# Seven block products for eight in the gate projection of four groups: a fused cosformer attention and SwiGLU kernel

## The chip, the cores and the metric

The kernel runs on one core of a Trainium2 chip. The time is device microseconds (us) of one execution, as the median of several runs. A profile of one execution stands beside it.

## The reference

Linear attention with cosine weights for 8 batches, 8 heads, 576 tokens and a head size of 64, followed by a gated feed-forward block of width 1536. In short:

```python
def phi(x, c, s):                      # c, s: cos and sin of pi/2 * position / 576
    r = np.maximum(x, 0.0)
    return np.concatenate([r * c, r * s], axis=-1)
kv  = einsum('bhsf,bhsd->bhfd', phi(k), v)
z   = sum over s of phi(k)
x   = einsum('bhsf,bhfd->bhsd', phi(q), kv) / (einsum('bhsf,bhf->bhs', phi(q), z) + 1e-6)
x   = x, heads side by side            # 4608 tokens x 512
g   = x @ w_gate                       # 512 x 1536
out = (g * sigmoid(g) * (x @ w_val)) @ w_out
```

All inputs and the output are float32.

## The kernel before

**Tiling.** The 4608 tokens go in nine groups (`tg` 0 to 8) of 512 tokens (T), each of four tiles of 128 tokens. For each group the kernel makes the normalised attention output x of four tiles, turns it into xT (512 features in four chunks of 128, tokens along the free axis), computes gate and value for twelve blocks of 128 hidden features (`fc` 0 to 11), and then the output projection of the group. x is held 4096 times too large (UP), and DOWN takes this out in silu and in the last copies.

**Engines.** Each engine executes its own queue strictly in the order in which the code issues instructions (`tc.manual_schedule`). Waits between engines follow from the data they share: PSUM banks, tiles, DMAs.

- TensorE: gate and value projections (`ffn_mm`, L535, eight matmuls of 512 columns for a block), the output projection, attention tiles (`a_tile2`, L419) and the sums over keys (`kv_mm`, L305).
- ScalarE: silu (`ffn_silu`, L541), relu of q and k (L238), some copies.
- VectorE: gate times value (`ffn_mul`, L546, into `ht`), the normalisation of a tile (`x_den`, `x_rec`, `x_mul`: L429, L438, L442), phi of q (`phi_q`, L255), weighted v (`vmul`, L259), copies.
- SP issues the transposing DMAs of q (`qturn_dma`) and of x to xT (`x_turn`, L519), and the stores. POOL issues the loads.

**The output projection** of groups 2 to 8 (`out_by_quarters`) is already done with seven block products for eight (Winograd's form): tokens and output features are halved, hidden features are split into the even and odd blocks, so each operand has four quarters. Four sums of weight quarters (`weight_sum`, T1 to T4) are made once, four sums of token quarters (`token_sum`, S1 to S4, L623) for each group. The seven products accumulate into banks a, b, c and e. b starts as ScalarE's copy of a; e goes to SBUF as C22; c starts as VectorE's sum of C22 and b.

**PSUM.** `take` and `give_back` share out the eight banks in program order. A request for one bank (`n = 1`) or an aligned pair (`n = 2`, for tiles and `kv_mm`) gets the free one that was used longest ago:

```python
b0 = min(free, key=lambda b: (n == 1 and hold is not None and hold[0] == "o" and b ^ 1 not in taken,
                              sorted(used[b:b + n], reverse=True)))
```

A request held under a name that begins with "o" prefers a bank whose neighbour is taken. A bank may be given again at once after `give_back`; the next writer then waits on the chip for the engine that still reads it. [...]

**Slots.** A group after the first two has 16 slots: one behind each `fc` and one at each of the four `slot_of` calls of the output projection. A plan (`at`) puts the attention work of coming groups into these slots: the four phi of the next batch at output slots 0, 0, 1, 2; the four `vmul` from output slot 3 to slot 2 of the next group; `kv_mm` at slot 5; the next group's tiles with their transposes at slots 5, 7, 9 and 11. Batch work ends with group 6, tiles with group 7. Group 8 has neither.

Of the kernel before, what the change touches and what calls it, by code (L numbers as in the profile page):

```python
# [10 lines left out]
FP32 = mybir.dt.float32  # L11
# [3 lines left out]
ALU = mybir.AluOpType  # L15
# [3 lines left out]
def kernel(  # L19
# [28 lines left out]
    HC = FC // 2  # L48
    HT = T // 2
    HD = d_model // 2  # L50

    consts = ctx.enter_context(tc.tile_pool(name="consts", bufs=1))
    raw = ctx.enter_context(tc.tile_pool(name="raw", bufs=3))
    rel = ctx.enter_context(tc.tile_pool(name="rel", bufs=1))
    phip = ctx.enter_context(tc.tile_pool(name="phip", bufs=2))
    xp = ctx.enter_context(tc.tile_pool(name="xp", bufs=4))
    xtp = ctx.enter_context(tc.tile_pool(name="xtp", bufs=3))
    smp = ctx.enter_context(tc.tile_pool(name="smp", bufs=3))
    sgp = ctx.enter_context(tc.tile_pool(name="sgp", bufs=5))
    obp = ctx.enter_context(tc.tile_pool(name="obp", bufs=2))  # L60
    psum = ctx.enter_context(tc.tile_pool(name="psum", bufs=1, space=bass.MemoryType.PSUM))

# [10 lines left out]
    def take(n, hold=None, fills=False, seeded=False):  # L73

        taken = {x for r in held.values() for x in r}
        free = [b for b in range(0, 8, n) if not any(b <= x < b + n for x in taken)
                and (filled[b] or not seeded)]

        b0 = min(free, key=lambda b: (n == 1 and hold is not None and hold[0] == "o" and b ^ 1 not in taken,
                                      sorted(used[b:b + n], reverse=True)))  # L80
        if hold is not None:
            held[hold] = range(b0, b0 + n)
        filled[b0:b0 + n] = [fills or seeded] * n
        touch(range(b0, b0 + n))
        return banks[:, b0] if n == 1 else banks[:, b0:b0 + n]
# [15 lines left out]

    def raw_of(b, nm):
        if (b, nm) not in raws:
            raws[b, nm] = raw.tile([P, G, NC, D], BF16, name=f"raw_{nm}")
        return raws[b, nm]

    def load(b, nm, parts=1):
# [48 lines left out]
    ident = consts.tile([P, P], BF16)  # L156
    make_identity(nc, ident)
    kvd = []
    for j in range(2):
        t = consts.tile([P, 8 * J * D1], BF16, name=f"kvd_{j}")  # L160
        if j:
            nc.gpsimd.memset(t.bitcast(FP32), 0.0)
        kvd.append(t.rearrange("p (e j w i x) -> p e j w i x", e=2, j=J, w=2, i=2))


    zeros = consts.tile([P, P], BF16)
# [41 lines left out]
        in_=csk.rearrange("p c e -> p (c e)").to_broadcast([P, NC * 2, D]),  # L208
    )
    v2s = []  # L210
    for j in range(2):
        t = consts.tile([P, G, NC, 2, W], BF16, name=f"v2_{j}")
        nc.vector.tensor_copy(out=t[:, :, :, :, D], in_=csk.unsqueeze(1).to_broadcast([P, G, NC, 2]))
        v2s.append(t)


    wg_sb = consts.tile([P, KC, d_ff], BF16)
    wv_sb = consts.tile([P, KC, d_ff], BF16)
    wg_r = moe_w_gate.rearrange("(c p) f -> p c f", p=P)
    wv_r = moe_w_val.rearrange("(c p) f -> p c f", p=P)  # L220
    wo_r = moe_w_out.rearrange("(c p) f -> p c f", p=P)
# [35 lines left out]

    def vmul(b, g):
        nc.vector.tensor_tensor(  # L259
            out=v2s[b % 2][:, g, :, :, 0:D],  # L260
            in0=(first if b == 0 and g == 0 else {"v": raw_of(b, "v")})["v"][:, g].unsqueeze(2).to_broadcast([P, NC, 2, D]),
            in1=tab, op=ALU.mult,
        )
# [34 lines left out]
    def kv_mm(b):  # L298
        ps = st[b, "kvps"] = take(2, ("kv", b))
        for j, c in [(j, c) for j in range(J) for c in range(NC)]:  # L300
            for i in range(2):
                for e in range(2):
                    es = slice(e * SH, (e + 1) * SH)
                    g = 2 * j + i
                    nc.tensor.matmul(  # L305
                        out=ps[i * D:(i + 1) * D, e, j * 2 * D1:(j + 1) * 2 * D1],
                        lhsT=raws[b, "k"][es, g, c],
                        rhs=v2s[b % 2][es, g, c, :, 0:D1],
                        start=(c == 0), stop=(c == NC - 1),
                    )  # L310

# [47 lines left out]
            give_back(("kvf", j))  # L359


    qf = consts.tile([P, 2, J, 2, D], BF16)
    qr = [lodge(4 * J * SH, BF16).rearrange("p (e j c s) -> p e j c s", e=2, j=J, c=2) for i in range(2)]
    qwT = [lodge(8 * J * SH, BF16).rearrange("p (w e j c s) -> p w e j c s", w=2, e=2, j=J, c=2) for i in range(2)]

# [68 lines left out]
    def x_rec(t, ps, ys=slice(0, 4)):  # L434
        if ys.start == 0:
            st["rec", t] = smp.tile([P, H, 1], FP32, name="rec")
            st["x", t] = xp.tile([P, d_model], BF16, name="x")
        nc.vector.reciprocal(out=st["rec", t].rearrange("p (e y) o -> p e y o", e=2)[:, :, ys],  # L438
                             in_=st["den", t].rearrange("p (e y) o -> p e y o", e=2)[:, :, ys])

# [40 lines left out]
    def x_norm(t):  # L481
        num = st.pop(("num", t)).rearrange("p j e (i x) -> p (j e i) x", i=2)
        den = smp.tile([P, H, 1], FP32, name="den")
        nc.vector.tensor_scalar(out=den, in0=num[:, :, D:D1], scalar1=1e-6, scalar2=DOWN,
                                op0=ALU.add, op1=ALU.mult)
        rec = smp.tile([P, H, 1], FP32, name="rec")
        nc.vector.reciprocal(out=rec, in_=den)
        x = xp.tile([P, d_model], BF16, name="x")
        for j in range(J):
            hs = slice(4 * j, 4 * j + 4)  # L490
            nc.vector.tensor_tensor(
                out=x[:, 4 * j * D:(4 * j + 4) * D].rearrange("p (i e d) -> p e i d", i=2, e=2),
                in0=num[:, hs, 0:D].rearrange("p (e i) d -> p e i d", e=2),
                in1=rec[:, hs].rearrange("p (e i) o -> p e i o", e=2).to_broadcast([P, 2, 2, D]), op=ALU.mult,
            )
        st["x", t] = x

    def xT_of(t):
        tg, off = divmod(t, GH // 2)
        if tg not in xT:  # L500
            xT[tg] = xtp.tile([P, GH // 2, KC, P], BF16, name="xT")
        return xT[tg][:, off]

    def x_turn_pe(t, ks=slice(0, KC)):
        ps = take(1, ("xt", t, ks.start)).bitcast(BF16).rearrange("p (k x) -> p k x", x=P)
        for kc in range(ks.start, ks.stop):
            nc.tensor.transpose(out=ps[:, kc], in_=st["x", t][:, kc * P:(kc + 1) * P], identity=ident)  # L507
        st["xt", t, ks.start] = ps[:, ks]

    def x_turned(t, eng, ks=slice(0, KC)):  # L510
# [40 lines left out]
    def ffn_act(*a):  # L551
        ffn_silu(*a)
        ffn_mul(*a)

    def ffn_fc(*a):

        ffn_mm(*a)
        ffn_act(*a)

    out_v = out.rearrange("(b p c) f -> b c p f", p=SH, c=NC)  # L560
    o_ps = {}
# [68 lines left out]
    def out_by_quarters(tg, slot_of):  # L630
# [60 lines left out]
        if last:  # L691
            store_two(t0 + 2, slice(HD, d_model))
        product(c, aq[:, 1, 1], T4, False)
        copied("dve", C21, c)
        free("c")
        if last:
            store_two(t0 + 2, slice(0, HD))
# [178 lines left out]
    for b in range(2, B):  # L876
        s0 = SLOTS * (b - 1)
        keng = "dve" if b == 2 else "act"
        steps = [lambda b=b, g=g: phi_q(b, g) for g in range(G)]
        steps += [lambda b=b, g=g: (relu_k(b, g, g + 1, keng), vmul(b, g)) for g in range(G)]  # L880
        if b == 2:
            fs, tq = [s0 + i for i in (0, 0, 1, 1, 4, 5, 5, 6)], (s0 + 2, s0 + 2)
        else:
            p0 = s0 - SLOTS
            fs, tq = [p0 + 12, p0 + 12] + [p0 + 11 + i for i in range(2, 8)], (p0 + 15, p0 + 16)
            if b == 3:
                fs, tq = [p0 + 12 + i for i in range(4)] + [s0 + 4, s0 + 4, s0 + 5, s0 + 5], (s0 + 2, s0 + 2)
            at(p0 + 3 if b < 5 else p0 + 1, lambda b=b: load_behind(b))
        tk = (s0 + 4, s0 + {2: 8, 3: 7}.get(b, 5))
        for s, f in zip(fs, steps):  # L890
            at(s, f)
        for e in range(2):
            at(tq[e], lambda b=b, e=e: qturn_dma(b, e))
        at(tk[-1], lambda b=b: kv_mm(b), lambda b=b: kv_out2(b))
        at(tk[-1] + 1, lambda b=b: kv_free(b))
    for t in range(2 * OUT, NTG * OUT):
        tg, i = divmod(t, OUT)
        s = SLOTS * (tg - 1) + (5 if tg > 2 else 4) + 2 * i
        if t == 2 * OUT:
            at(s, a_(t, 0))  # L900
            at(s + 1, a_(t, 1), turn(t))
        elif tg == 2:
            at((9, 10, 11)[i - 1] + SLOTS, lambda t=t: a_tile2(t), turn(t))
            if i == 2:
                at(11 + SLOTS, load_3)
        else:
            if t in (13, 14, 15):
                s = SLOTS * 2 + t - 4
            at(s, lambda t=t: a_tile2(t), turn(t))
    for tg in range(1, NTG):  # L910
        s0 = SLOTS * tg
        for fc in range(FC):
            ffn_fc(tg, fc)
            if tg > 1:
                sums_behind(fc)
            slot(s0 + fc)
        if tg > 1:
            out_by_quarters(tg, lambda i: slot(s0 + FC + i))
            continue
        for i in range(OUT):  # L920
            ffn_out(tg * OUT + i)
            weight_sum(i)
            slot(s0 + FC + i)
# [31 lines left out]
```

## Time and profile before

| what | us |
|---|---|
| median of 3 runs (lowest, highest) | 318.22 (317.78, 318.86) |
| the profiled execution | 317.96 |
| its span in the profile | 316.2 |
| TensorE busy | 309.1 (98%) |
| VectorE busy | 220.2 (70%) |
| ScalarE busy | 134.1 (42%) |
| granted TensorE clock | 1.0 throughout |

In the profile's rows PE is TensorE's matmuls, PEld its weight loads, DVE is VectorE, ACT ScalarE. A row gives line, engine, operation, output and input tiles with shapes, the busy time and the mean of one, and the idle time before it with the engine that ended it. A matmul's row includes its drain, so consecutive matmuls overlap; their rate is read from the starts. The chain of waits follows the work that ended last back to its releasers.

### The profile page before, as it was taken

To read this page: it belongs to the slowest core of one execution; us is meant where nothing else is said; L and a number is where in the kernel's file an instruction comes from. 1 tells how busy PE (TensorE), PEld (TensorE's weight loads), DVE (VectorE), ACT (ScalarE), POOL (GpSimd) and SP (SyncE) were. 2 spreads that over 40 slices of the span, in tenths; PEclk is the share of its full clock that TensorE was granted. 3 is DMA by queue.
4 is the path that set the end of the run, shared out by engine and by line. 5 is a ranking of instruction groups with operands and counts; after the bars stand their busy time and mean duration, and the time that the engine had idled before them with its cause. 6 is when DMAs were issued, how large, how long until landed. Compare 5 with 4: busy or idle time off the path is not lost.

```text
span 316.2 us, 6614 instructions
## 1 busy us (share of the span) xinstructions
PE 309.1 (98%) x2624; PEld 182.7 (58%) x2624; DVE 220.2 (70%) x441; ACT 134.1 (42%) x245; POOL 35.5 (11%) x60
## 2 busy tenths in 40 slices
PE   8899999999999999999999999999999999999994
PEld 4596555455445485548554765477456745774473
DVE  7873777797658888597858785879578437743652
ACT  7554545753435354335433453344433133213330
POOL 6754102000201100030003000300000000000000
PEclk9999999999999999999999999999999999999999
DMA  7999999998796985979795979598951241133004
GB/s 259 220 198 197 206 205 139 226 130 110 140 225 88 175 116 135 129 80 197 148 142 75 200 149 145 72 199 134 157 77 35 58 93 23 39 69 72 2 0 133
DMA packets 74766, 41.06 MB, mean 130 GB/s; under 512 B 49904, under 2 KB 69872, under 8 KB 74736
## 3 DMA queue, kind: packets, MB, share of 16 engines
q1 hardware_dynamic: 51952, 22.55, 39.7%
q0 software_dynamic: 22192, 17.57, 37.1%
q10 hardware_dynamic: 592, 0.52, 0.5%
q8 instruction: 20, 0.33, 0.4%
q14 instruction: 10, 0.08, 0.1%
HBM read 37.75 MB, written 9.44 MB: 149 GB/s over the span
## 4 chain that ended last, share of the span: by engine, by line
PE 86%; DVE 6%; DMA 4%; ACT 2%; issue 1%; DVEq 0%; ACTq 0%
PE banks L535 57%; PE banks L649 15%; PE banks L592 6%; DMA xT<-x 4%; PE banks L305 3%; PE banks L419 2%; DVE ht L546 1%; DVE sums L623 1%; DVE x L442 1%; PE banks L465 1%; PE banks L401 1%; DVE v L259 1%; PE banks L172 1%; PE banks L345 0%; PE banks L507 0%
## 5 line engine op out<-in xcount | busy, mean ns | idle before, releaser
L541 ACT ACTIVATE sg<-banks 128x512 bf16<-128x512 f32 (+2 forms) x116 | 65.8, 568 | 118.7 <-PE banks L535 115.6
L535 PE MATMUL banks<-xT,wg_sb 128*128 128x512 bf16 (+2 forms) x464 | 111.3, 364 | 0.3 <-DMA xT<-x 0.2
L535 PE MATMUL banks<-xT,wv_sb 128*128 128x512 bf16 (+2 forms) x464 | 111.3, 364 | 0.0
L546 DVE TENSOR_TENSOR ht<-sg,banks 128x512 f16<-128x512 bf16 (+2 forms) x116 | 74.5, 648 | 52.2 <-PE banks L535 45.5
L535 PEld LDWEIGHTS <-wv_sb 128*128 128x128 bf16 x464 | 44.9, 98 | 48.7
L535 PEld LDWEIGHTS <-wg_sb 128*128 128x128 bf16 x464 | 43.0, 98 | 42.3 <-issue 0.4
L649 PEld LDWEIGHTS <-ht 128*128 128x128 f16 x336 | 32.4, 98 | 3.9
L649 PEld LDWEIGHTS <-sums 128*128 128x128 f16 x252 | 24.6, 98 | 3.6 <-issue 0.8
L259 DVE TENSOR_TENSOR v<-raw_v,tab 128x1152 bf16<-128x1152 bf16 x31 | 22.7, 751 | 0.3 <-ACT raw_v L712 0.3
L592 PE MATMUL banks<-wo_sb,ht 128*128 128x512 f16 x96 | 22.7, 379 | 0.0
L442 DVE TENSOR_TENSOR x<-banks,rec 128x512 bf16<-128x512 f32 (+1 forms) x32 | 21.6, 674 | 1.3 <-PE banks L401 0.3
L649 PE MATMUL banks<-wo_sb,ht 128*128 128x256 f16 x168 | 20.6, 273 | 0.0
L649 PE MATMUL banks<-wt_sb,sums 128*128 128x256 f16 x168 | 19.5, 273 | 0.0
L649 PE MATMUL banks<-wt_sb,ht 128*128 128x256 f16 x168 | 19.5, 273 | 0.0
L255 DVE TENSOR_TENSOR r_q<-raw_q,tab 128x1152 bf16<-128x1152 bf16 x24 | 17.6, 752 | 2.4 <-ACT raw_q L238 2.1
L238 ACT ACTIVATE raw_k<-raw_k 128x576 bf16<-128x576 bf16 (+1 forms) x25 | 17.0, 694 | 0.0
L861 POOL COPY hold<-phit 1x2 bf16<-1x2 bf16 x5 | 1.2, 234 | 130.4 <-DMA phit<-r_q 130.4
L623 DVE TENSOR_TENSOR sums<-ht 128x1024 f16<-128x1024 f16 (+1 forms) x28 | 15.5, 552 | 0.2
L238 ACT ACTIVATE raw_q<-raw_q 128x576 bf16<-128x576 bf16 x24 | 15.0, 674 | 0.0
L592 PEld LDWEIGHTS <-ht 128*128 128x128 f16 x96 | 9.1, 98 | 8.9 <-issue 0.2
L419 PEld LDWEIGHTS <-phit 128*128 128x128 bf16 (+1 forms) x240 | 10.0, 100 | 6.5 <-issue 1.3
L664 DVE TENSOR_SCALAR ob<-banks 128x512 f32<-128x512 f32 (+1 forms) x15 | 9.8, 656 | 4.4 <-PE banks L649 3.6
(98 smaller groups left out, 223.9 us busy)
## 6 DMA issues: line engine op xcount, KB each, us to landing
out_dram<-ob SPq DMA_DIRECT2D x67, 128.0 KB, 2.4
raw_k<-in_k_dram POOLq DMA_DIRECT2D x7, 576.0 KB, 9.0
raw_q<-in_q_dram POOLq DMA_DIRECT2D x6, 576.0 KB, 6.5
raw_v<-in_v_dram POOLq DMA_DIRECT2D x6, 576.0 KB, 11.7
wo_sb<-in_moe_w_out_dram POOLq DMA_DIRECT2D x3, 512.0 KB, 12.8
wg_sb<-in_moe_w_gate_dram POOLq DMA_DIRECT2D x5, 256.0 KB, 9.0
wv_sb<-in_moe_w_val_dram POOLq DMA_DIRECT2D x5, 256.0 KB, 9.3
wo_sb<-in_v_dram SPq DMA_DIRECT2D x2, 576.0 KB, 4.1
```

The costliest lines, as they stand in the source:

```text
L238: nc.scalar.activation(out=out, in_=in_, func=AF.Relu)
L255: nc.vector.tensor_tensor(out=st[b, "q"][:, g], in0=o.unsqueeze(2).to_broadcast([P, NC, 2, D]), in1=tab, op=ALU.mult)
L259: nc.vector.tensor_tensor(out=v2s[b % 2][:, g, :, :, 0:D], in0=(first if b == 0 and g == 0 else {"v": raw_of(b, "v")})["v"][:, g].unsqueez ...
L419: nc.tensor.matmul(out=ps[ms, e, g * D1:(g + 1) * D1], lhsT=phit[b][:, e, g, c:c + n].rearrange("p c s -> p (c s)"), rhs=kv2s[b % 2][:, e, ...
L442: nc.vector.tensor_tensor(out=st["x", t].rearrange("p (y e d) -> p e y d", e=2, d=D)[:, :, ys], in0=ps[:, :, 0:2 * J * D1].rearrange("p e ...
L535: nc.tensor.matmul(out=st["f", tg, fc, lo][i], lhsT=(wg_sb, wv_sb)[i][:, kc, fs], rhs=xT[tg][:, ts, kc], start=(kc == 0), stop=(kc == KC - 1))
L541: nc.scalar.activation(out=sg[:, 0:n], in_=st["f", tg, fc, lo][0], func=AF.Silu, scale=DOWN)
L546: nc.vector.tensor_tensor(out=ht[:, fc, r:r + n], in0=st.pop(("s", tg, fc, lo))[:, 0:n], in1=ps[1], op=ALU.mult)
L592: nc.tensor.matmul(out=o_ps[t], lhsT=ht[:, fc, r:r + P], rhs=wo_sb[:, fc], start=(fc == 0), stop=(fc == FC - 1))
L623: nc.vector.tensor_tensor(out=o[:, lo:hi], in0=x[:, lo:hi], in1=y[:, lo:hi], op=op)
L649: nc.tensor.matmul(out=to[i][:, 0] if len(to) == 2 else to[0][:, i], lhsT=a[:, kc, i * P:(i + 1) * P], rhs=b[:, kc], start=first and kc == ...
L664: nc.vector.tensor_single_scalar(out=o_, in_=p_, scalar=x, op=ALU.mult)
```

## The change

The gate projection of groups 5 to 8 (`GATE`) is done with the same seven products. Hidden features are split into even and odd blocks (w), the 512 input features into two halves, tokens into two halves. Four sums of quarters of `w_gate` (W1 to W4) are made once, one at the last slot of each of groups 1 to 4. Four sums of quarters of xT (X1 to X4) are made for each group at the last two slots of the group before. A group runs u = 0, 1, 2, and in each u 28 matmuls of 256 columns for four gate blocks, with the value blocks V (unchanged: four matmuls of 512 columns each) in between.

Around it: weights, x and xT become FP16 for BF16; tiles of groups 6 to 8 move to slots 1, 2, 4, 7 (group 8: 1, 2, 5, 6); the copy C21 of the output projection moves from VectorE to ScalarE in every group; `take` prefers half-free pairs for "g" and "v" as well where fewer than three pairs are whole; raw k and v have two buffers for three; W1 to W4 and X1 to X4 lie in memory of tiles used early (`wgs_sb` over the second v tile and `qf`, `xs_sb` over `kvd`).

```diff
-    raw = ctx.enter_context(tc.tile_pool(name="raw", bufs=3))
+    raw = ctx.enter_context(tc.tile_pool(name="raw", bufs=2))
+    rawq = ctx.enter_context(tc.tile_pool(name="rawq", bufs=3))
...
+        whole = sum(b not in taken and b + 1 not in taken for b in range(0, 8, 2))
+        b0 = min(free, key=lambda b: (n == 1 and hold is not None and b ^ 1 not in taken and
+                                      (hold[0] == "o" or hold[0] in "gv" and whole < 3),
                                       sorted(used[b:b + n], reverse=True)))
...
+    wg4 = wg_sb.rearrange("p (k c) (u w x) -> p w k c u x", k=2, w=2, x=P)
+    A11, A12, A21, A22 = wg4[:, 1, 0], wg4[:, 1, 1], wg4[:, 0, 0], wg4[:, 0, 1]
...
+    def gate_weight_sum(n):
+        o, x, y, op = ((W1, A21, A22, ALU.add), (W2, W1, A11, ALU.subtract), (W3, A11, A21, ALU.subtract),
+                       (W4, A12, W2, ALU.subtract))[n]
+        nc.vector.tensor_tensor(out=o, in0=x, in1=y, op=op)
+    def x_sum(tg, n):
+        B11, B12, B21, B22 = x_parts(tg)
+        o, x, y = ((X1, B12, B11), (X2, B22, X1), (X3, B22, B12), (X4, B21, X2))[n]
+        nc.vector.tensor_tensor(out=o, in0=x, in1=y, op=ALU.subtract)
...
+        def V(u, i, w):
+            fc = 4 * u + 2 * i + w
+            val[u, i, w] = take(1, ("v", tg, fc), fills=True)
...
+        for u in range(3):
+            a = bank("a", fills=True)
+            product(a, u, A11, B11, True)
+            b = bank("b", seeded=True)
+            nc.scalar.copy(out=b, in_=a)
+            e = bank("e", fills=True)
+            product(e, u, W3, X3, True)
+            m7 = m7p.tile([P, 2, HT], FP32, name="m7")
+            nc.scalar.copy(out=m7, in_=e)
+            free("e")
+            V(*((u - 1, 1, 1) if u else (u, 0, 0)))
+            done()
+            product(b, u, W2, X2, False)
+            c = bank("c", seeded=True)
+            nc.vector.tensor_tensor(out=c, in0=m7, in1=b, op=ALU.add)
+            product(a, u, A12, B21, False)
+            silu(u, 1, 0, a)
+            free("a")
+            if u:
+                mul(u - 1, 1, 1)
+            V(u, 0, 0) if u else V(u, 1, 0)
+            done()
+            product(b, u, W1, X1, False)
+            nc.vector.tensor_tensor(out=m7, in0=m7, in1=b, op=ALU.add)
+            silu(u, 0, 1, m7)
+            product(c, u, A22, X4, False)
+            silu(u, 0, 0, c)
+            free("c")
+            V(u, 1, 0) if u else V(u, 0, 1)
+            done()
...
+            mul(u, 0, 0)
+            mul(u, 1, 0)
...
+            product(b, u, W4, B22, False)
+            silu(u, 1, 1, b)
+            free("b")
+            if u:
+                V(u, 0, 1)
+            mul(u, 0, 1)
...
+        V(2, 1, 1)
+        mul(2, 1, 1)
...
-        copied("dve", C21, c)
+        copied("act", C21, c)
...
+    for n in range(4):
+        at(SLOTS * (1 + n * (GATE[0] - 1) // 4) + FC + 3, lambda n=n: gate_weight_sum(n))
+    for tg in GATE:
+        for n in range(4):
+            at(SLOTS * (tg - 1) + FC + (2, 2, 3, 3)[n], lambda tg=tg, n=(2, 0, 1, 3)[n]: x_sum(tg, n))
...
+            elif tg - 1 in GATE:
+                s = SLOTS * (tg - 1) + ((1, 2, 7, 9) if tg < 6 else (1, 2, 4, 7) if tg < 8 else (1, 2, 5, 6))[i]
...
+        if tg in GATE:
+            ffn_by_quarters(tg, lambda i: slot(s0 + i))
```

`product` issues four matmuls of 256 columns (two blocks i, two chunks c); `silu` is one ScalarE operation over 2 x 256 columns, `mul` one VectorE operation over 512; `done` runs the next slot of the plan.

## The prediction

> **What bounds the kernel now.** I read the page's busy rows first, then the chain of work that ended last over the second half, then the stage windows, then the timeline at one group boundary. The page and the chain:
>
> ```profile
> PE 309.1 (98%) x2624; PEld 182.7 (58%) x2624; DVE 220.2 (70%) x441; ACT 134.1 (42%) x245; POOL 35.5 (11%) x60
> 250.77 10.36 PE banks L535 x48
> ...
> 272.52 9.17 PE banks L649 x84
> 281.69 20.72 PE banks L535 x96
> 302.41 9.18 PE banks L649 x84
> ```
>
> TensorE is never short of work. In group 8, 96 matmuls of 512 columns take 20.72 us, 216 ns each, and 84 of 256 columns take 9.18 us, 109 ns each, with nothing in between. So weight loads are hidden at both sizes. The windows of groups 4 to 7 (us from:to and length, then PE, PEld, DVE, ACT busy):
>
> ```profile
> 152.80:185.40 32.60, 32.55 (x292) 19.55 (x292) 24.68 (x46) 14.26 (x25) 2.41 (x4) 1.00 0.86 140
> 185.40:218.00 32.60, 32.40 (x285) 19.53 (x284) 24.61 (x47) 14.25 (x25) 2.70 (x4) 1.00 0.89 140
> 218.00:250.50 32.50, 32.50 (x296) 19.69 (x294) 22.30 (x43) 11.40 (x20) 0.00 (x0) 1.00 0.50 86
> 250.50:283.00 32.50, 32.50 (x222) 19.43 (x220) 19.24 (x37) 9.35 (x16) 0.00 (x0) 1.00 0.25 54
> ```
>
> VectorE has 8 us to spare in groups 4 and 5, 13 in group 7. The timeline at the start of group 6 gives the hand-over times:
>
> ```profile
> 217.48 0.75 DVE L255 TENSOR_TENSOR r_q<-raw_q,tab 128x1152 bf16<-128x1152 bf16 x1
> 218.17 1.03 PE L535 MATMUL banks<-xT,wg_sb 128*128 128x512 bf16 x4
> 218.37 0.69 DVE L664 TENSOR_SCALAR ob<-banks 128x512 f32<-128x512 f32 x1
> 218.98 0.75 DVE L259 TENSOR_TENSOR v<-raw_v,tab 128x1152 bf16<-128x1152 bf16 x1
> 219.03 1.03 PE L535 MATMUL banks<-xT,wv_sb 128*128 128x512 bf16 x4
> 219.23 0.60 ACT L541 ACTIVATE sg<-banks 128x512 bf16<-128x512 f32 x1 [2.67 <-PE banks L535]
> ```
>
> The gate matmuls end at 219.03, where the next begin; silu starts 0.20 us later and takes 0.60. On VectorE a 0.69 us operation is followed by the next after 0.61 (218.37 to 218.98), since tails overlap. TensorE waiting for an engine shows early in the trace, in the chain:
>
> ```profile
> 38.66 1.29 PE banks L305 x71
> ...
> 40.77 0.92 ACT phit L353
> 41.69 0.04 issue
> 41.73 0.64 PE banks L465 x8
> ```
>
> So TensorE starts 0.04 us after the operation it waits for. A bank that must be emptied by ScalarE straight after the product that filled it holds TensorE for 0.20 + 0.60 + 0.05 = 0.85 us.
>
> **What is removed and added on TensorE.** Per group 48 gate matmuls of 512 columns (10.36 us) become 3 x 7 products of four 256-column matmuls, 84 x 109 ns = 9.17: 1.19 us less, 4.77 over four groups. FP16 for BF16 costs nothing: the FP16 L592 matmul of 512 columns has a mean of 379 ns, as L535 has in BF16.
>
> **The waits that come instead.** Call a value block V(u,i,w) (0.86 us) and a product P (0.44 us). The order of instructions, and `take` followed through its calls for the bank numbers, show where TensorE waits. With fewer than three bank pairs whole, `take` gives a V the half-free pair.
>
> Group 8, the lightest (no tiles, no batch work), from its first matmul at 0: a, e, V, b+W2X2, a+A12B21 end at 2.61. The next instruction is V(0,1,0), in the bank that a just left, so it waits for silu of a: 0.85. Then b+W1X1 ends at 4.76 and c at 5.20. V(0,0,1) takes c's bank. ScalarE runs silu of m7 ahead of silu of c, and m7 waits for VectorE's add of b: 4.76 + 0.20 + 0.69 + 0.04 + 0.49 (ScalarE's step from a 0.60 us row to the next, 211.63 to 212.12) + 0.60 + 0.05 = 6.83, a wait of 1.63. V(1,1,0) is again in a's bank (0.85), and so is V(2,0,0) (0.85). Group 8: 4.2 us.
>
> Group 7 has four tiles. The first stands between V(0,1,0) and b+W1X1; its den, rec and x (1.04 us together on VectorE, 231.62 to 232.67 in the timeline) stand ahead of the m7 add, which can start at 5.82 and not 5.22: the wait for c's bank becomes 2.23. V(0,1,1) reuses the bank of V(0,0,1), freed by the third of three multiplies (0.60 each) that queue behind the second tile: TensorE is ready at 10.1, the multiply ends at 11.94, a wait of 1.87. V(1,1,1) waits 0.75 in the same way. With 0.85 twice for a's bank: 6.55 us.
>
> Groups 5 and 6 have batch work as well, and their first products wait for the new token sums. C21 now goes to ScalarE, ahead of the fourth relu of q. It cannot start before the product ends (1.30 us before the group), so relu ends at -0.13 and r_q runs from -0.09, not -0.69. X3 follows it and ends at 1.07, but product e wants it at 0.44: 0.68 us. Then VectorE has X1, C12 (0.61), one v (0.74) and X2, which ends at 3.12, 0.75 later than b+W2X2 could start; in group 5 W4 lies ahead as well (0.95 by L614's row of the same size, 0.87 where an operation follows it): 1.62. From there as group 7, except the bank of V(1,1,1): e and V of u = 2 wait 0.79 and 0.77 since VectorE stood idle for ScalarE's kv copy, and the c add comes 0.25 late behind a tile. Group 6: 9.0; group 5: 9.9.
>
> VectorE cannot catch up there: to 24.6 us in group 5 come six adds (3.7) and four X sums (1.4) less C21 (0.6), 29.1 of the 31.2 us left for the group. Its c and m7 adds from PSUM have no row of their own; I take L679 and L690 (0.69). The floor for one is the 0.42 of the 512-element FP16 sum, the top 0.95.
>
> **Edits that I cost at nothing.** W1 to W3 (0.95 each) end groups 1 to 3, where VectorE's multiplies of a group wait 4.3 us for TensorE; uncovered 2.9 in all. X sums in groups 7 and 8 end at 1.23, ahead of 1.74. The tiles' transposes on SP (3.0 us each, after 8 us of phit) land some 7 us ahead of the sums; if not, X3 is late by the difference. Two raw_k and raw_v buffers for three: the work they wait for (L305 of two batches before) is done a group earlier. The second identity costs POOL 0.5 us, inside its 1.8 us wait for v. Six copies per group on ScalarE (0.57) leave it near 60% busy. The shared tiles (kvt, wgs_sb) were last read by group 1.
>
> **Sum.** 9.9 + 9.0 + 6.55 + 4.2 = 29.7 of waits, less 4.77, is +24.9 us. On the profiled execution (317.96 us, span 316.2) that makes 342.9, and the median of the runs is 0.26 above it: 343.1, say 343.
>
> [...]
>
> On the clock: TensorE stood still from 39.95 to 41.73, 1.8 us, and that window shows a granted clock of 1.00. My longest wait is 2.2, so I keep full clock. [...]
>
> **Rivals.**
> (1) Only the fixed waits remain: a's bank nine times (7.65) and c's bank at its least, four times 1.63 (6.5); X sums, multiplies and tiles are in time. 14.2 - 4.8 = +9.4: 327.6. For it: VectorE's lag is the softest part of my sum. Against: VectorE at 93% in group 5. Chance 0.14.
> (2) Faster: TensorE isn't held, because the emptied banks are free by the time it arrives. It decides where the waits of one group stay under 1.19 us. Then up to 4.77 is gained: 313.4. For it: the same seven-product scheme of the output runs without gaps (84 in 9.17). Against: that one empties its banks behind products of 1.31 us; here the V stands directly behind, and two hand-overs of 0.85 already exceed 1.19. Chance 0.04, and 0.01 that it ends within 0.3% (about what a measurement of this kernel can tell from no change).
> (3) Slower still: VectorE's operations in groups 5 and 6 step at 0.69 and not 0.61: some 35 in each x 0.08 = 5.6 more, or the clock drops in the waits: 349 and up. Chance 0.07 for over 351.
> The forecast has the remaining 0.74, with 334 to 351 its own range. To keep 8 in 10 I go down to 327, where (1) lies. Faster 0.04, same 0.01, slower 0.95.
>
> **What would show it.** TensorE's busy share falls to near 89%. Its largest waits are V behind the silu (sg2) by ScalarE, about 16 us in total with singles of 0.85 and 1.6 to 2.2, and V behind the multiplies on VectorE, about 8. Groups 1 to 4 keep their length, up to the few tenths of C21. Group 8 is 3 us longer, group 5 near 9. I am wrong if products of group 8 run without gaps at a's and c's banks, or if the waits of a group stay under 1.2 us.

## The result, and the profile after

The changed kernel takes 343.61 us (median of 4 runs, 343.25 to 344.28), the kernel before 318.54 beside it (317.78 to 318.92). The ratio is 1.0793, 95% interval 1.0764 to 1.0821. The profiled execution took 343.82, its span is 342.0. The forecast was 343.0.

The page's busy rows, with the granted clock in 40 slices of the span:

```profile
PE 311.4 (91%) x2768; PEld 197.6 (58%) x2768; DVE 238.5 (70%) x478; ACT 149.9 (44%) x276; POOL 35.9 (10%) x62
PE   7999999999999999999998588985889779997994
PEclk9999999999999999999999989999999989999999
```

No engine is full any more. TensorE has 144 matmuls more than before, each smaller, and its share fell from 98% to 91%. From slice 22 on it dips once in each of the four groups, down to 5 in groups 5 and 6 and to 7 in groups 7 and 8; the slices ahead are full but for the first. Twice the clock is a digit lower; that was not foreseen and comes back below.

TensorE's waits from 185 us to the end (line waited at, releaser's line, us in total, times, longest):

```profile
PE banks L620 <- ACT sg L614: 14.3, 13, 2.1
PE banks L620 <- DVE ht L625: 5.0, 6, 1.7
PE banks L608 <- DVE kvt L592: 2.7, 4, 1.3
PE banks L608 <- DVE ht L625: 1.3, 2, 0.6
```

L620 is a value block V, L608 a product of the gate. L614 is silu, L625 the multiply, L592 the X sums, and further down L655 is the add that makes m7, L458 a tile's x, L435 a tile's matmuls, L773 the output projection and L747 its token sums. Each idle time is counted from the modelled end of the last matmul, which is about 0.16 us later than its successor could have started (in the profile before a row of 512 columns has a mean of 379 ns, and the starts are 216 ns apart); so 14.3 of idle in 13 waits is 16.4 of lost time.

The chain of work that ended last, at the start of group 8 (start, length, what):

```profile
306.19 0.89 PE banks L608 x8
307.10 0.61 ACT sg L614
307.71 0.04 issue
307.75 1.02 PE banks L620 x4
308.78 0.45 PE banks L608 x4
309.25 0.70 DVE m L655
309.99 0.04 issue
310.03 1.12 ACT sg L614 x2
311.15 0.04 issue
311.20 1.02 PE banks L620 x4
```

Before, this place was one row of 96 matmuls. Now the chain leaves TensorE twice in 5 us. First: product a ends, silu of a (0.61) empties its bank, and V follows 0.04 later. Then: b ends, VectorE makes m7 (0.70), ScalarE does silu of m7 and only then silu of c (1.12 for both), and the V that wants c's bank starts.

The four groups in the windows view (from:to and length; then PE, PEld, DVE, ACT, POOL busy; granted clock; DMA share; GB/s):

```profile
185.20:226.40 41.20, 34.15 (x323) 23.68 (x321) 29.89 (x57) 17.95 (x33) 2.41 (x4) 0.96 0.66 111
226.40:266.70 40.30, 32.81 (x330) 22.92 (x328) 27.61 (x54) 15.47 (x28) 0.00 (x0) 1.00 0.40 70
266.70:304.30 37.60, 32.32 (x251) 22.69 (x249) 22.92 (x45) 12.42 (x22) 0.00 (x0) 0.95 0.20 43
304.30:337.40 33.10, 29.49 (x218) 20.90 (x215) 19.25 (x34) 12.21 (x23) 0.00 (x0) 1.00 0.18 44
```

Set against the prediction (a group's length goes from its first gate matmul to that of the next group, for group 8 to the end of the output; forecast = length before + waits − 1.19):

| group | before | forecast | after | difference |
|---|---|---|---|---|
| 5 | 32.39 | 41.10 | 41.24 | +0.14 |
| 6 | 32.43 | 40.24 | 40.31 | +0.07 |
| 7 | 30.92 | 36.28 | 37.59 | +1.31 |
| 8 | 29.89 | 32.90 | 33.08 | +0.18 |

### The profile page after: what moved, and what is told of

It is laid out like the page before. It is cut to its first block, busy times and chain, and to the rows that moved or that the text cites. A ratio compares the mean times of both kernels' runs of the same rounds, so it can differ in the third digit from the quotient of the medians.

```text
span 342.0 us, 6928 instructions
## 1 busy us (share of the span) xinstructions
PE 311.4 (91%) x2768; PEld 197.6 (58%) x2768; DVE 238.5 (70%) x478; ACT 149.9 (44%) x276; POOL 35.9 (10%) x62
## 4 chain that ended last, share of the span: by engine, by line
PE 80%; DVE 11%; ACT 6%; issue 2%; ACTq 0%; DVEq 0%
PE banks L551 31%; PE banks L773 18%; PE banks L620 11%; PE banks L608 7%; PE banks L716 6%; ACT sg L614 4%; DVE ht L625 3%; PE banks L435 2%; DVE x L458 2%; PE banks L320 2%; DVE m L655 1%; DVE v L274 1%; PE banks L481 1%; PE banks L417 1%; DVE kvt L592 1%
## 5 line engine op out<-in xcount | busy, mean ns | idle before, releaser
L620 PE MATMUL banks<-xT,wv_sb 128*128 128x512 f16 x192 | 49.4, 383 | 19.3 <-ACT sg L614 14.3
L551 PE MATMUL banks<-xT,wg_sb 128*128 128x512 f16 (+2 forms) x272 | 62.0, 354 | 0.0
L551 PE MATMUL banks<-xT,wv_sb 128*128 128x512 f16 (+2 forms) x272 | 62.0, 354 | 0.0
L557 ACT ACTIVATE sg<-banks 128x512 bf16<-128x512 f32 (+2 forms) x68 | 37.2, 547 | 53.4 <-PE banks L551 51.3
L562 DVE TENSOR_TENSOR ht<-sg,banks 128x512 f16<-128x512 bf16 (+2 forms) x68 | 41.5, 620 | 22.5 <-PE banks L551 15.5
L551 PEld LDWEIGHTS <-wv_sb 128*128 128x128 f16 x272 | 26.1, 98 | 26.1
L620 PEld LDWEIGHTS <-wv_sb 128*128 128x128 f16 x192 | 18.8, 98 | 36.2 <-issue 23.3
L551 PEld LDWEIGHTS <-wg_sb 128*128 128x128 f16 x272 | 25.0, 98 | 21.8
L773 PEld LDWEIGHTS <-ht 128*128 128x128 f16 x336 | 32.7, 98 | 4.6
L625 DVE TENSOR_TENSOR ht<-sg,banks 128x512 f16<-128x512 bf16 x48 | 31.1, 680 | 3.4 <-ACT sg L614 3.3
L614 ACT ACTIVATE sg<-banks 128x512 bf16<-128x512 f32 x36 | 20.8, 591 | 27.7 <-PE banks L608 27.6
L773 PEld LDWEIGHTS <-sums 128*128 128x128 f16 x252 | 24.3, 98 | 4.5 <-DVE sums L747 0.9
L608 PE MATMUL banks<-kvt,wgs_sb 128*128 128x256 f16 x144 | 22.1, 277 | 4.1 <-DVE kvt L592 2.7
L608 PEld LDWEIGHTS <-wgs_sb 128*128 128x128 f16 x192 | 18.2, 100 | 13.0 <-issue 3.5
L458 DVE TENSOR_TENSOR x<-banks,rec 128x512 f16<-128x512 f32 (+1 forms) x32 | 21.6, 674 | 1.3 <-PE banks L417 0.3
L773 PE MATMUL banks<-wo_sb,ht 128*128 128x256 f16 x168 | 20.6, 273 | 0.0
L614 ACT ACTIVATE sg<-m 128x512 bf16<-128x512 f32 x12 | 7.6, 630 | 28.7 <-DVE m L655 28.7
L773 PE MATMUL banks<-wt_sb,sums 128*128 128x256 f16 x168 | 20.0, 273 | 0.0
L773 PE MATMUL banks<-wt_sb,ht 128*128 128x256 f16 x168 | 19.5, 273 | 0.0
```

What stands on the lines that cost most here:

```text
L458: nc.vector.tensor_tensor(out=st["x", t].rearrange("p (y e d) -> p e y d", e=2, d=D)[:, :, ys], in0=ps[:, :, 0:2 * J * D1].rearrange("p e ...
L551: nc.tensor.matmul(out=st["f", tg, fc, lo][i], lhsT=(wg_sb, wv_sb)[i][:, kc, fs], rhs=xT[tg][:, ts, kc], start=(kc == 0), stop=(kc == KC - 1))
L557: nc.scalar.activation(out=sg[:, 0:n], in_=st["f", tg, fc, lo][0], func=AF.Silu, scale=DOWN)
L562: nc.vector.tensor_tensor(out=ht[:, fc, r:r + n], in0=st.pop(("s", tg, fc, lo))[:, 0:n], in1=ps[1], op=ALU.mult)
L608: nc.tensor.matmul(out=to[:, i], lhsT=a[:, c, 2 * u + i], rhs=x[:, :, c], start=first and i == 0 and c == 0, stop=c == KH - 1, skip_group_ ...
L614: nc.scalar.activation(out=gates[u, w][:, :, j * HT:(j + 1) * HT], in_=src, func=AF.Silu, scale=DOWN)
```

## The experiments

The theory: TensorE's waits, not its matmuls, set the time; most of them come from the choice of banks, and a smaller part from VectorE. Rivals: VectorE is the limit whatever the banks are, or the other edits cost the time.

### Another bank choice: e1_rotate

```diff
-                                      (hold[0] == "o" or hold[0] in "gv" and whole < 3),
+                                      (hold[0] == "o" or hold[0] in "gv" and whole < 2),
```

> Changed kernel with `whole < 2` for `whole < 3` in take: a V no longer gets the bank that the product right before it filled. Theory (bank choice): the 0.85 us waits for a's bank (nine), the 1.6 to 2.2 us waits for c's bank (four) and the waits of V(0,1,1) behind three multiplies go; left are the X sums, a tile ahead of e and the kv copies in groups 5 and 6 (about 4.7 and 3.8 us), 0.6 in group 7 and none in group 8, which should last 28.8 us. Sum 343.6 - 22 = about 322 us. Rival (VectorE and ScalarE have too much work in these groups, whichever bank is used): no more than 3 us faster, 340 or above. No change of the computation.

Measured 322.43 us (322.15 to 322.71), ratio 1.0122 (1.0099 to 1.0144). One digit takes 21.2 us off the changed kernel. TensorE's waits from 185 us on:

```profile
PE banks L608 <- DVE kvt L592: 2.7, 4, 1.4
PE banks L608 <- DVE x L458: 1.7, 3, 0.7
PE banks L608 <- DVE ht L625: 1.2, 2, 0.6
PE banks L773 <- DVE ht L625: 0.8, 1, 0.8
```

Every wait at L620 is gone, those behind silu and those behind multiplies alike. What stays in these rows is VectorE alone: X sums, a tile's x, multiplies. The X sums' 2.7 us are as before the edit, so that term does not depend on banks. The groups take 35.53, 34.58, 30.76 and 29.65 us. Against their length before less 1.19, group 5 is still 4.3 too long, group 6 3.3, groups 7 and 8 1.0 each. Group 8 had been expected at 28.8 us without a wait; its output waits 0.79 for a multiply. (In e6, e7 and e8 below, where the other choice holds for banks of the output too, group 8 has no such wait.) So both are true: the banks make most of the loss, and without them a smaller loss by VectorE remains. Group 7 is 0.16 us shorter here than with eight products.

### The order of two silu: e2_silu_c_first

```diff
-            silu(u, 0, 1, m7)
             product(c, u, A22, X4, False)
             silu(u, 0, 0, c)
             free("c")
+            silu(u, 0, 1, m7)
```

> Changed kernel with silu of c issued ahead of silu of m7 on ScalarE, banks as they were. Theory: the wait for c's bank falls to one hand-over, 0.85 us, in each group (0.8 less in group 8, 1.4 less in groups 5 to 7), so 4.9 us less, and up to 2.6 more if the slow stretch of TensorE after a 2.1 us wait goes with it: 336 to 339 us. Rival (ScalarE's and VectorE's amount of work): the same work in another order, 343.6 within 1 us.

Measured 338.09 us (337.84 to 338.14), ratio 1.0612 (1.059 to 1.0634): 5.5 us less than the changed kernel. The first two waits of TensorE:

```profile
PE banks L620 <- ACT sg L614: 9.1, 13, 0.7
PE banks L620 <- DVE ht L625: 6.8, 6, 1.7
```

Still 13 waits behind silu, but none over 0.7: in c's bank too V now waits for the silu alone. So the 1.6 to 2.2 at c's bank were the m7 add and the silu of m7 ahead of it in their queues, as the sum had it (its terms, 1.63 and three times 2.23, would fall to 0.85 each, 4.9 in all). The waits for multiplies grow from 5.0 to 6.8, all of it at V(0,1,1) in groups 5 and 7: there the changed kernel ran at a low clock (0.63 and 0.55 in the windows of the last section), which delayed TensorE itself and hid part of the wait (0.45 and 1.15 of idle time, here 1.70 in both). What was gained beyond 4.9 may come from that clock, which is 1.00 in the windows of all four groups here.

### C21 back on VectorE: e3_c21_dve

```diff
-        copied("act", C21, c)
+        copied("dve", C21, c)
```

> Changed kernel with C21 copied by VectorE again. Theory: the fourth r_q starts 0.6 us earlier at the starts of groups 5 and 6, X3 and X2 with it, and the wait before product e there falls from 0.6-0.7 to 0.1 us; groups 7 and 8 stay: 1.2 us less, 342.4 us. Rival (VectorE's load sets groups 5 and 6): 0.6 us more VectorE work per group makes it 1.2 us or more slower, 344.8 or above.

Measured 342.77 us (342.05 to 344.41), ratio 1.0768 (1.073 to 1.0805), 0.84 below the changed kernel where 1.2 was expected. The two intervals overlap, so this difference alone shows little; the waits say more. Of the four waits at X sums that for X3 in group 6 is gone, that in group 5 falls from 0.45 to 0.15, and one is now put down to ScalarE's relu of k. So the moved copy makes X3 late, as the sum had it, and explains little of the 25 us.

### No products, all else kept: e5_none

```diff
-    GATE = (5, 6, 7, 8)
+    GATE = ()
```

The weight sums are spread as for the four groups.

> Changed kernel with no group in the list: gate projection as before in all groups, but with everything around it (FP16 weights and x, C21 on ScalarE, the rule of take, two raw k and v buffers, W sums made and not used, tiles at their old slots). Theory: within 0.5 us of the kernel before, 318.0 to 319.1 us. Rival (the edits around it cost): 2 us or more above it.

Measured 317.74 us (317.55 to 318.07), ratio 0.9976 (0.9965 to 0.9987). This falls below what was expected, by 0.3 us: the edits around the products don't cost a little, they gain 0.65 us. FP16, C21 on ScalarE, two buffers, weight sums and shared memory were tried only together. Before, the first gate matmul of group 5 waited 0.2 for the DMA of xT, and here it doesn't; where the rest lies is open. For the question at hand it settles that all of the loss belongs to the products and what goes with them.

### The products in one group: e4_group8

```diff
-    GATE = (5, 6, 7, 8)
+    GATE = (8,)
```

> Seven products in group 8 alone, with the bank choice of the changed kernel; the computation is the same. Theory (the waits lie in each group and add up): groups 5 to 7 as before, group 8 longer by its own waits of 4.2 us less the 1.19 us saved, so 317.7 (the kernel with eight products in every group) + 3.1 = 320.9 us, and waits of TensorE behind silu of 4.2 us in all. Rival (the waits come only with the attention work of groups 5 to 7, group 8 was long only because it inherited a late VectorE): 318 us or less.

Measured 320.79 us (320.55 to 320.9), ratio 1.0078 (1.006 to 1.0096). Group 8 is 2.87 longer than with eight products. Its four waits, from TensorE's timeline (start, length, engine, line, operation; in brackets the idle time and its releaser):

```profile
284.89 1.02 PE L620 MATMUL banks<-xT,wv_sb 128*128 128x512 f16 x4 [0.68 <-ACT sg L614]
288.27 1.02 PE L620 MATMUL banks<-xT,wv_sb 128*128 128x512 f16 x4 [1.49 <-ACT sg L614]
293.03 1.02 PE L620 MATMUL banks<-xT,wv_sb 128*128 128x512 f16 x4 [0.69 <-ACT sg L614]
297.80 0.60 PE L608 MATMUL banks<-kvt,wgs_sb 128*128 128x256 f16 x4 [0.27 <-DVE ht L625]
```

With 0.16 added to each, the three behind silu are 0.84, 1.65 and 0.85, against 0.85, 1.63 and 0.85 in the sum. The sum had a third 0.85, which does not show; a wait of 0.43 behind a multiply stands instead. The waits belong to the group and add up: the rival, that group 8 was long only because VectorE came late into it, is out.

### The same with the other bank choice: e8_gate8_rotate

```diff
-    GATE = (5, 6, 7, 8)
+    GATE = (8,)
...
-                                      (hold[0] == "o" or hold[0] in "gv" and whole < 3),
+                                      hold[0] in "gvo" and whole < 2,
...
```

Unlike in e1, the choice holds for "o" as well. The kernel also has the tile slots of e6 below, which nothing uses here, since no tiles are made in group 8.

> Seven products in group 8 alone, and g and v (as o) take half-free pairs only where fewer than two pairs are whole; the computation is the same. Theory (without the waits at emptied banks the whole saving of 1.19 us is kept, since nothing else competes for VectorE in group 8): 317.74 - 1.19 = 316.55 us, no waits of TensorE in group 8 before the output. Rival (the X sums and adds still cost something there): 317.4 us or above.

Measured 316.79 us (316.67 to 316.94), ratio 0.9964 (0.9951 to 0.9976): faster than the kernel before. The chain in group 8:

```profile
281.73 0.87 PE banks L608 x8
282.60 0.86 PE banks L620 x4
...
299.53 1.73 PE banks L620 x8
301.26 9.32 PE banks L773 x84
```

It never leaves TensorE in the group. Group 8 takes 28.84 us where eight products take 29.89: 1.05 saved of the 1.19 in the sum. The rest is 0.14 in the output (9.32 for 9.18). So the saving on TensorE was real and nearly of the size worked out, and in group 8 the bank choice alone turned it into a loss. Of all versions this has the lowest median; by their ratios e6, e11 and e12 below can't be told from it. (Its ratio is only 0.0012 below that of e5, where 1.05 us would be 0.0033; the two were timed on different chips, and their intervals allow for either.)

### Two and three groups: e6_gate78, e7_gate678

The first has `GATE = (7, 8)`, the bank choice of e8 and

```diff
-                s = SLOTS * (tg - 1) + ((1, 2, 7, 9) if tg < 6 else (1, 2, 4, 7) if tg < 8 else (1, 2, 5, 6))[i]
+                s = SLOTS * (tg - 1) + (1, 4, 6, 8)[i]
```

> Seven products in groups 7 and 8 only, requests of o, g and v alike prefer half-free pairs only where fewer than two pairs are whole, and the tiles of group 8 stand at slots 1, 4, 6, 8 of group 7; the computation is the same. Theory (the loss was the bank choice and the crowding of tiles, the saving on TensorE is real): 317.74 - 2 x 1.19 = 315.4 us, no waits of TensorE behind silu; group 7 near 29.8 us from first gate matmul to the first of group 8. Rival (added VectorE work gives new waits that eat the saving): 317.4 us or above.

Measured 317.18 us (316.87 to 317.28), ratio 0.9962 (0.9947 to 0.9976). Better than before, but not the 315.4 of the theory; the rival's 317.4 is nearer. Group 8 again takes 1.05 less, and group 7 takes 31.26 where eight products take 30.92. It lost its 1.19 and 0.34 more. VectorE in the last third of group 7 (its timeline):

```profile
268.40 0.69 DVE L458 TENSOR_TENSOR x<-banks,rec 128x512 f16<-128x512 f32 x1
269.01 0.68 DVE L655 TENSOR_TENSOR m<-m,banks 128x512 f32<-128x512 f32 x1
269.61 0.68 DVE L747 TENSOR_TENSOR ht<-ht 128x1024 f16<-128x1024 f16 x1
```

The tile's x stands ahead of the m7 add, which must read b before product W4B22 may write there; TensorE waits for it until 269.74. From 263.35 to 275.38 VectorE's timeline shows no idle time.

The other has group 6 as well:

```diff
-    GATE = (5, 6, 7, 8)
+    GATE = (6, 7, 8)
...
+    for n in range(4):
+        at(SLOTS * (GATE[0] - 1) + FC + (1, 1, 2, 2)[n], lambda n=(2, 0, 1, 3)[n]: x_sum(GATE[0], n))
...
```

with the bank choice of e6, tiles of groups 7 and 8 at (1, 4, 6, 8), those of group 6 at (1, 3, 7, 9), and the kv copies of batch 7 one slot later.

> As the kernel with groups 7 and 8, with group 6 as well: its X sums stand one output slot earlier in group 5, ahead of phi, its tiles at slots 1, 3, 7, 9, and the kv copies of batch 7 one slot later; the computation is the same. Theory (group 6 too can keep its saving if VectorE's work is spread): 314.3 to 315.2 us, below the kernel with two groups. Rival (VectorE is too full beside batch work, so the first products wait for the X sums and the multiplies): 316.3 us or above, and slower than the kernel with two groups.

Measured 320.97 us (320.03 to 322.63), ratio 1.0085 (1.0057 to 1.0112): the rival holds. The cause is in part its own. VectorE and TensorE at the end of group 5, each from its timeline:

```profile
217.29 0.76 DVE L592 TENSOR_TENSOR kvt<-xT 128x512 f16<-128x512 f16 x2 [1.56 <-DMA xT<-x]
218.63 0.68 DVE L814 SCALAR_TENSOR_TENSOR ob<-banks,ob 128x512 f32<-128x512 f32 x1
```

```profile
219.37 1.72 PE L773 MATMUL banks<-wo_sb,sums 128*128 128x256 f16 x12 [2.18 <-DVE ob L814]
```

The X sums, issued a slot earlier, held VectorE 1.56 us until the transposes of the last tile had landed; an add of the output (L814) queued behind them, and TensorE behind that. Whether group 6 could gain in another order is therefore not shown.

### Where group 7's tiles go: e9_tiles_behind_m7, e11_tiles_0346, e12_tiles_0134

Each is e6_gate78 with other slots for the tiles: (2, 5, 6, 9), (0, 3, 4, 6) and (0, 1, 3, 4) for (1, 4, 6, 8).

> Seven products in groups 7 and 8 as in the kernel with these two, and the tiles of group 8 at slots 2, 5, 6, 9, so that their den, rec and x stand behind the add of m7 on VectorE and not ahead of it; the computation is the same. Theory (what group 7 lost were the three waits of W4B22 for the m7 add, 0.24, 0.30 and 0.47 us, and one of the output for its sums): 317.18 - 1.0 = 316.2 us, or 315.7 if the sums come in time as well. Rival (VectorE's work is late whatever its order, the waits move to the multiplies and sums): 317 us or above.

> Seven products in groups 7 and 8, tiles of group 8 at slots 0, 3, 4, 6 of group 7, none in its last third; the computation is the same. Theory (the waits of group 7 come from a VectorE that has no idle time in the last third of the group, from 263 us on, so tiles must be done before): the wait of the third W4B22 (0.47) and of the sums (0.48) go, those of the first go with the slot, 0.30 at slot 4 stays: 317.18 - 1.2 = 316.0 us. Rival (VectorE is short in the whole group, the waits only move to the multiplies and c adds of the first two thirds): 317 us or above.

> As the kernel before it with the tiles at slots 0, 1, 3, 4, all in the first half; the computation is the same. Theory: 316.0 us or a few tenths less, with at most the two waits of W4B22 for the m7 add of the first two blocks (0.24 and 0.30 us). Rival (four tiles in half a group crowd VectorE, and c adds and multiplies come late): 317 us or above.

Measured: 318.32 us (317.84 to 318.92, ratio 1.0007, 0.9996 to 1.0017); 317.2 (317.08 to 317.8, ratio 0.996, 0.9947 to 0.9973); 317.26 (317.07 to 318.24, ratio 0.9969, 0.9957 to 0.9981). All three expected about 1 us of gain on e6 and none has it. Group 7 takes 32.55, 31.52 and 31.58. TensorE's waits of e9, then of e12:

```profile
PE banks L773 <- DVE ht L625: 0.9, 2, 0.6
PE banks L773 <- DVE sums L747: 0.5, 1, 0.5
```

```profile
PE banks L435 <- DVE ht L625: 0.7, 1, 0.7
PE banks L608 <- DVE m L655: 0.3, 1, 0.3
```

In e9 the waits for the m7 add are gone, and the output waits for multiplies and sums. With the tiles early the output comes in time, and a tile's banks wait for a multiply. In each order the waits are VectorE's and only their place changes; none of the four orders brings group 7 under the 30.92 of eight products. So the theory that one bad order made the waits has fallen, for these orders. That VectorE's added work must cost that much in every order is not shown. The shortest group 7 measured is that of e1, 30.76, with its tiles at slots 1, 2, 5, 6 and the banks of "o" chosen as in the changed kernel; these slots were not tried with the choice of e8.

### A second profile of the changed kernel: e10_after_again

> The changed kernel once more, for a second profile of its granted clock. If the low clock comes from the long waits, it stands again behind waits of 2.1 us in groups 5 to 7, and nowhere else in them; if it has another cause, it may stand at any other place. Time 343.6 us.

343.29 us, with the same waits (14.3 us behind silu in 13). The low clock stands behind only one of its three waits of 2.1 us, in group 7 (0.60 from 274.50 to 278.20 us), and nowhere else in groups 5 to 8 (0.99 or 1.00 in every other window from 185 to 337 us); the last section says more.

## Why the prediction was right, step by step

**The saving.** 1.19 us per group; e8 shows 1.05 of it where no wait covers it.

**The bank choice.** The fixed terms held. a's bank 0.85: measured 0.84 and 0.85 in e4, 0.85 to 0.90 in the changed kernel. c's bank in group 8 1.63: 1.65. c's bank behind a tile 2.23: 2.25 to 2.31 (idle of 2.09 to 2.15 and 0.16). V behind the third multiply 1.87: 1.86 in group 6 and, in e10, in groups 5 and 6; in the first profile 0.61 in group 5 and 1.31 in group 7, where the low clock (0.63 and 0.55) had already delayed TensorE. All terms at emptied banks together were some 22 us in the sum; e1 takes away 21.2.

So the choice of banks has a price of 21.2 of 343.61 us here. The 313.4 of rival (2) allows for no wait at all and was not reached in any run: VectorE's waits keep e1 at 322.43.

**VectorE.** X3 before e in group 5 0.68 forecast, 0.61 measured (product e could start at 185.59 and started at 186.20). X2 in group 5 1.62 forecast, 1.51 measured:

```profile
186.20 0.60 PE L608 MATMUL banks<-kvt,wgs_sb 128*128 128x256 f16 x4 [0.45 <-DVE kvt L592]
189.01 0.61 PE L608 MATMUL banks<-kvt,wgs_sb 128*128 128x256 f16 x4 [1.35 <-DVE kvt L592]
```

VectorE's busy time in group 5 was forecast as 29.1 and is 29.89, with the W4 sum (0.95), which that list of terms left out. Its steps of 0.61 were right (an operation of 0.69 at 186.40 is followed by the next at 187.00); rival (1), fixed waits alone, is refuted by e1's remaining waits, rival (2) by e4. Of rival (3) the clock came true (0.63 and 0.55 behind two of the waits), at a far smaller price than it set.

**What was off.** Two terms, with opposite signs. The prediction kept full clock, and its length for group 7 is 1.31 short of the profiled one. And "groups 1 to 4 keep their length" was wrong by a little: group 5 starts at 185.15 in this profile and 185.38 in e10, against 185.78 before. The four differences of the table add up to 1.70, the earlier start takes off 0.63 and the work behind the last matmul 0.16; that is the 0.9 between the 342.9 of the sum and the 343.82 of the profiled execution. The median moved less; not every run pays the whole of group 7's 1.31, as e10 shows (36.94 in group 7, 343.29 in all). That the forecast comes so near is in part luck, since the two cancel in part. TensorE's share was forecast near 89% and is 91%. An estimate: each of the 25 waits leaves 0.16 us of drain uncovered, 4.0 us in all, and the low clock adds some 2 (311.4 us of rows against 309.4 in e2).

Full clock had no ground in the trace. The prediction took 39.95 to 41.73 of the profile before for a time in which TensorE stood still. Only the chain leaves TensorE there; TensorE goes on with other matmuls and is busy for 3.05 of the 3.10 us around it:

```profile
38.70:41.80 3.10, 3.05 (x92) 2.31 (x91) 2.82 (x6) 2.33 (x5) 0.00 (x0) 1.00 1.24 207
```

TensorE's longest wait in that profile is 1.0 us, so it says nothing of the clock behind one of 2.

## What to carry to other kernels

Count what a scheme with fewer products takes besides matmuls: here each group saves 1.19 us on TensorE and adds six adds and four sums on VectorE and six copies on ScalarE, so here it paid where VectorE had room, as in group 8 (1.05 us), and brought 0.16 us at best in the orders tried where tiles are made at the same time, as in group 7. When accumulators are read by other engines, follow the allocator by hand to the bank that the next matmul takes: here a bank just handed over cost the whole hand-over (0.84 to 0.90 us behind one silu, 1.65 to 2.31 where more operations queued ahead). And before a loss is put down to the new work, try the other choice of banks; it was one digit and 21 us.

## What the runs showed of the hardware that was not expected

The granted clock fell after some waits of little over 2 us. Windows of the changed kernel in groups 5 and 7, each time the stretch that ends with the wait, then the one behind it:

```profile
190.00:195.00 5.00, 2.23 (x22) 1.44 (x21) 3.67 (x8) 2.35 (x5) 0.00 (x0) 1.00 0.97 147
195.00:198.50 3.50, 3.50 (x23) 2.41 (x23) 1.96 (x5) 1.32 (x3) 0.00 (x0) 0.63 1.00 145
270.00:274.50 4.50, 2.16 (x20) 1.43 (x20) 1.65 (x4) 1.28 (x3) 0.00 (x0) 0.99 0.62 138
274.50:278.20 3.70, 3.68 (x22) 2.17 (x22) 1.27 (x4) 0.49 (x1) 0.00 (x0) 0.55 0.02 3
```

The same two places in the second profile, e10:

```profile
195.00:198.50 3.50, 2.59 (x24) 1.82 (x24) 1.91 (x5) 1.49 (x4) 0.00 (x0) 1.00 0.90 129
274.50:278.20 3.70, 3.64 (x23) 2.35 (x23) 1.89 (x5) 0.75 (x3) 0.00 (x0) 0.60 0.03 6
```

What it does to a value block, from the timeline of the changed kernel, behind the same wait in groups 6 and 7:

```profile
235.46 1.02 PE L620 MATMUL banks<-xT,wv_sb 128*128 128x512 f16 x4 [2.15 <-ACT sg L614]
274.52 1.86 PE L620 MATMUL banks<-xT,wv_sb 128*128 128x512 f16 x4 [2.14 <-ACT sg L614]
```

In the three profiles with these waits (the changed kernel twice, and e3) the idle time is 2.08 to 2.15 in groups 5, 6 and 7. The clock fell behind it in group 7 in all three (0.55, 0.60 and 0.57 from 274.50 to 278.20), in group 5 in one (0.63), in group 6 in none (1.00 from 236 to 241). In e7 it fell to 0.66 for 3.5 us behind one wait of 2.18 with TensorE busy throughout the 5 us ahead. In e1, e2, e4, e6, e8, e9, e11 and e12, whose waits in groups 5 to 8 are of 1.7 or less, the windows read in these groups show 1.00, and the mean clock of the profiled executions is 0.996 to 1.0. In windows of 0.5 us of the changed kernel the clock stands at 0.50 from 196.0 to 199.0 and from 274.5 to 277.5, with a part of a window at either end. The price of a fall is not the doubled matmul time: group 5 of the two profiles takes 41.24 with it and 41.06 without, because the next wait shrinks (1.70 at V(0,1,1) in e10, 0.45 here). In group 7, where no profile is without it, the length is 36.8 to 37.6 against 36.28 forecast at full clock.

Full clock had been expected at waits of 2.2 us. What decides between groups 5, 6 and 7 was not tested. Behind the same wait in group 5 (2.09 us of idle time here, 2.08 in e10) the clock is 0.63 in one profile and 1.00 in the other, so the length of the wait alone does not decide it.
